# Heads of a delta-rule attention packed as 64-row blocks, with one PSUM bank per head, and another backward pass in the scheduler

## The chip, the cores and the metric

The kernel runs on one core of one Trainium2 chip. The metric is the device time of one launch in microseconds, the median of 3 runs. The engines are PE (TensorE; PEld is its weight loading), DVE (VectorE), ACT (ScalarE), POOL (GpSimd) and SP (SyncE, which issues all the DMAs here).

## What is computed

A delta-rule attention over 4 x 8 heads of 768 tokens and 48 features, then two MLPs over the 3072 tokens, 384 to 2048 to 384 features. Everything is float32.

```python
def _attn_ref(q, k, v, beta):
    k_n = k / (np.linalg.norm(k, axis=-1, keepdims=True) + 1e-06)
    state = np.zeros((B, H, D, D))
    for t in range(S):
        kt, vt, bt = k_n[:, :, t], v[:, :, t], beta[:, :, t, None]
        y[:, :, t] = np.einsum('bhd,bhde->bhe', q[:, :, t], state)
        v_old = np.einsum('bhde,bhd->bhe', state, kt)
        state = state + bt[..., None] * np.einsum('bhd,bhe->bhde', kt, vt - v_old)

def _moe_ref(x, w_in, w_out):
    h = x @ w_in
    return np.where(h > 0, h, np.exp(np.minimum(h, 0)) - 1) @ w_out

def _moe2_ref(x, w_in, w_out, a, b):
    h = x @ w_in
    P = a[0] + a[1] * h + a[2] * h**2 + a[3] * h**3
    Q = 1 + abs(b[0]) * abs(h) + abs(b[1]) * h**2
    return (P / (Q + 1e-06)) @ w_out
```

## The kernel before

**The attention** works in 12 steps of 64 tokens, two steps to a window (WINS, 6 windows). A step has 32 heads, in two halves `hf` of 16. In a half, 8 columns `u` times two heads `h` lie in the partitions, and the 64 tokens of a head are two blocks of 32. Per step the small PE groups are these (the names in bold are those of the profile):

- **gp** (`g_item`, 4 items per window): the products k·k and k·q of a head, 32 matmuls of 48 rows by 32 columns, 128 wide. DVE masks out `p`; three ACT copies per half put the diagonal blocks into `gd` and the block below the diagonal into `lo`.
- The inversion of the 32 x 32 triangles on DVE (`t_pieces`): a transpose `am<-gd`, the norms, then a chain of a product into `tmp` and a sum out of it (`merge`), and a transpose into `tp_t`, once per window for 32 blocks in 128 partitions.
- **ks** (64 matmuls of 48 x 32): the state times k; DVE subtracts it from `kv`, which POOL has scaled (`prep`), into `R`.
- **cb** three times: `solve(0)` with `tp_t`, `lo` with the block below the diagonal, `solve(1)`. ACT copies between them, DVE subtracts.
- `u2`: ACT copies the solution twice per half into `ub`, each time through a mask `mh_sb` that keeps one of two heads; `s_bd`, the state, has a block of zeros beside each head's state for the same reason.
- **y** (`yy`, per half): 8 matmuls of 128 x 64, 96 wide, with the state and 8 with `ub`, into one bank; a copy `y1`, three transposes **xt** (`xx`), and a copy into `xs`.
- **ku** (per half, 16 matmuls of 128 x 48): the update of the state, which DVE adds into `s_bd` by head.

The attention's PSUM tiles come from one ring of three banks, `pa`; a tile waits until the one three places ahead of it was read.

**The MLPs** are PE groups of 9 matmuls of 128 x 128, 512 wide (kind `F` in the code; `h`, `h_a`, `h_b`, `h_c` and `o` in the profile). The first MLP runs by windows, `H` and `O` of 16 feature tiles, among which the small groups of the next window are put; then the second MLP has PE to itself. `split_x` makes the high and low part `xh` and `xl` of a window's `xs`, and the window's first `H` waits for them. The weights come as float64 words and are converted on ACT, DVE and POOL (`conv_x`, `conv_d`, `conv_s`: the DVE operations `wo<-wo` and `ce<-wo`, 192 wide, of the first 140 us).

**What sets the order.** Every operation is recorded with its dependencies; `order` then runs a list scheduler over them, whose `simulate` has tables of durations (`PEC`, `LEAVE`, `ENTER`, `PAIR` for PE's groups, `SLACK` for the DMAs), and whose `backward` hands back to the next round how late an operation may be. The best of 8 rounds is written out as a fixed order for each engine. While PE waits ahead of the first F group, `gaps` puts matmuls named `fill` (L1478) into its queue, as many as the scheduler thinks fit; they have no dependency, but what stands behind them waits for them. `start` issues the first loads: `gin` tiles (two DMAs each, 48 partitions, 2 KB runs) for gp, then the rest.

In the profile all recorded operations have line 193, that of the recorder's `emit`, so tiles are read by their names.

Of the kernel before, what the change touches and what calls it, by code (L numbers as in the profile page):

```python
# [20 lines left out]
D = 48  # L21
NSC = 12
# [8 lines left out]
NV = 7  # L31
# [5 lines left out]
    wm1=6, wk=4, wr=3, wr0=4)  # L37


class View:  # L40
# [62 lines left out]

    def real(self):
        a = self.base.get()
        for c in self.chain:
            if c[0] == "[]":
# [67 lines left out]
class Recorder:  # L175
    def __init__(self, nc):
        self.nc, self.ops, self.group, self.live = nc, [], None, False
# [81 lines left out]
    def dma(self, out, in_):  # L259
        v = out if isinstance(out, View) else in_  # L260
        n = v.ids.size * 4 * (v.part[1] - v.part[0])
        self.add("SP", self.nc.sync.dma_start, dict(out=out, in_=in_), [out], [in_], SLACK["issue"], 2000, n)
# [44 lines left out]
    "F": (226.7, 425), "gp": (27.3, 475), "ks": (13.4, 330), "so": (22, 220), "lo": (22, 250), "yy": (85, 262), "ku": (47, 263),  # L307
    "xx": (90, 405), "wm": (200, 500), "yt": (33, 260)}
LEAVE = {"F": 2040, "so": 774, "lo": 812, "ks": 960, "gp": 970, "ku": 855, "yy": 1471, "xx": 290, "wm": 500, "yt": 1400}
ENTER = {"F": 0, "so": 71, "ks": 71, "xx": -25, "ku": 70, "yy": 20, "gp": 60, "lo": 100, "wm": 50, "yt": 20}  # L310
PAIR = {
# [3 lines left out]
SIZE = {"F": 9, "yy": 16, "yt": 48}  # L315
SLACK = {"small": 150, "F": 100, "x": 30, "issue": 560, "rate": 240, "land": 2300, "wait": 1500, "space": 3900, "room": 290, "first": 432, "hold": 400, "jit": 300, "pj": 0}
MIX = [
    (1076044, 1), (92414181, 200), (90150106, 200), (77610261, 20), (97147800, 60), (84287398, 200),
    (75730493, 60), (8425654, 600),
]  # L320

# [15 lines left out]
def order(ops, rounds):  # L337
# [17 lines left out]
    for _ in range(rounds):  # L355
# [3 lines left out]
        backward(ops, end)  # L359
# [5 lines left out]
def gaps(first):  # L365
    out, last = {}, None
    for o in first:
# [3 lines left out]
        if g.kind == "F":  # L371
            break
        if last is not None:
            n = len(last.ops) / SIZE[last.kind] if last.kind in SIZE else 1.0
            idle = o.start - last.ops[0].start - pe_cost(last.kind, "gp") * n - 300
            if idle > 430 and o.start > 20000:
                out[o] = int(idle / 430)
        last = g
# [7 lines left out]
def simulate(ops):  # L386
# [96 lines left out]
    while done < total:  # L483
# [10 lines left out]
        if e == "PE":  # L494
# [8 lines left out]
            if mode is not None:  # L503
                stop = began + pe_cost(mode, u.kind) * size
                t = max(t, stop)
                if u.kind == "F":
                    fill = False
                clock(began, t if fill else stop, t)
                if fill and t > max(stop, 20000) + 500:
# [4 lines left out]
                    while count > SLACK["first"] + 254.6 * used[0]:  # L514
                        used[0] += 1
            mode, began = u.kind, t
# [30 lines left out]
def backward(ops, end):  # L547
    nxt = end
    for o in sorted(ops, key=lambda o: (-o.start, -o.n)):
# [4 lines left out]
        if o.eng == "PE":  # L554
            late = nxt = min(late, nxt - o.pitch)
# [6 lines left out]
def kernel(  # L562
    ctx: ExitStack,
    tc: tile.TileContext,
    c_kq: bass.AP,
# [3 lines left out]
    mask_h: bass.AP,  # L569
# [988 lines left out]
```

## Time and profile before

| | |
|---|---|
| median of 3 runs (lowest, highest) | 1002.0 us (1001.04, 1003.21) |
| the profiled execution: its time, its span | 1002.51 us, 1000.7 us |
| PE busy | 982.7 us (98%), 10402 matmul records |
| DVE, ACT, POOL busy | 846.6, 753.1, 382.5 us |
| mean granted TensorE clock | 0.997 |
| DMA | 96.77 MB, mean 97 GB/s |

The span is the time from the first to the last instruction of the profiled execution; 1.8 us of its time lie around it. A float32 matmul has two records on PE, so a group of 32 shows x64; the F groups' matmuls have one each. A row of the timeline merges instructions of one kind that follow each other: its first number is the start, its second the time from there to the end of the last. Since PE's matmuls overlap, the time that a group takes is best read from its start to the next group's start. All the rows stand in their own section below.

### The profile page before, as it was taken

How to read it: one execution, taken by the hardware profiler on the slowest of the kernel's cores; microseconds unless marked ns; L12 is line 12 of the kernel's file. 1: busy time of each engine (PE TensorE's matmuls, PEld its weight loads, DVE VectorE, ACT ScalarE, POOL GpSimd, SP SyncE). 2: the span in 40 equal slices, each digit the busy share in tenths (PEclk: the TensorE clock that was granted, in tenths of full speed). 3: DMA queues.
4: the chain of work that ended last, by engine and by line, in shares of the span. 5: the costliest groups of instructions: out<-in, count | busy, mean ns of one | idle time of the engine just before them, and what ended most of it. 6: DMA issues, size and time to landing. Idle time of an engine off the chain costs nothing.

```text
span 1000.7 us, 25423 instructions
## 1 busy us (share of the span) xinstructions
PE 982.7 (98%) x10402; PEld 801.3 (80%) x10402; DVE 846.6 (85%) x1218; ACT 753.1 (75%) x1524; POOL 382.5 (38%) x282
## 2 busy tenths in 40 slices
PE   6999999999999999999999999999999999999997
PEld 4877878877887887788888888888888888888885
DVE  3999969987995998799666477889999999999996
ACT  3779799887877887887788778676676676766763
POOL 2353546542331242223222244364363643633332
PEclk9999999999999999999999999999999999999998
DMA  9554074226426432641545932001010010000000
GB/s 236 141 166 156 20 216 140 64 82 209 139 66 184 146 115 77 183 139 64 163 121 187 357 125 79 1 23 42 0 64 1 1 64 1 32 1 0 32 1 31
DMA packets 61588, 96.77 MB, mean 97 GB/s; under 512 B 7072, under 2 KB 39968, under 8 KB 61472
## 3 DMA queue, kind: packets, MB, share of 16 engines
q1 hardware_dynamic: 61472, 95.15, 30.4%
q8 instruction: 81, 1.33, 0.6%
q14 instruction: 35, 0.29, 0.1%
HBM read 73.11 MB, written 22.02 MB: 95 GB/s over the span
## 4 chain that ended last, share of the span: by engine, by line
PE 95%; DVE 2%; ACT 1%; issue 1%; DMA 0%; SPq 0%; ACTq 0%; DVEq 0%
PE o L193 39%; PE h L193 19%; PE h_b L193 10%; PE h_a L193 9%; PE fill L1478 4%; PE cb L193 3%; PE y L193 3%; PE gp L193 3%; PE ku L193 1%; PE ks L193 1%; PE h_c L193 1%; PE xt L193 1%; ACT wo L193 1%; DVE wo L193 1%; DMA wo<-c_kq 0%
## 5 line engine op out<-in xcount | busy, mean ns | idle before, releaser
L193 POOL TENSOR_TENSOR wor<-wo,wor 128x384 fp32r<-128x384 f32 x96 | 114.9, 1199 | 283.9 <-ACT wor L193 260.3
L193 POOL TENSOR_TENSOR gl<-wo 128x1024 fp32r<-128x1024 f32 x47 | 138.8, 2953 | 189.1 <-DVE wo L193 142.8
L193 PE MATMUL o<-gh,wor 128*128 128x512 f32 x576 | 195.1, 396 | 0.0
L193 PE MATMUL h<-xh,wi 128*128 128x512 f32 x546 | 185.5, 398 | 0.0
L193 ACT ACTIVATE wo<-wo 128x1024 f32<-128x1024 f32 (+3 forms) x224 | 142.3, 672 | 41.9 <-DVE wo L193 37.8
L193 PE MATMUL o<-gh,wo 128*128 128x512 f32 x576 | 139.7, 391 | 0.0
L193 PEld LDWEIGHTS o<-gh,wor 128*128 128x128 f32 x576 | 108.1, 188 | 23.9 <-issue 0.2
L193 PEld LDWEIGHTS o<-gh,wo 128*128 128x128 f32 x576 | 108.9, 189 | 22.7
L193 PEld LDWEIGHTS h<-xh,wi 128*128 128x128 f32 x546 | 102.4, 188 | 23.1 <-issue 0.6
L193 PE MATMUL o<-gl,wor 128*128 128x512 f32 x288 | 112.2, 390 | 0.0
L193 PE MATMUL h<-xl,wi 128*128 128x512 f32 x273 | 106.4, 390 | 0.3 <-DVE xl L193 0.3
L193 DVE SCALAR_TENSOR_TENSOR e<-e,pe 128x512 f32<-128x512 f32 x96 | 74.4, 775 | 37.4 <-ACT e L193 36.6
L193 DVE SCALAR_TENSOR_TENSOR wo<-wo 128x192 int32<-128x192 int32 (+2 forms) x101 | 87.4, 869 | 17.9 <-ACT wo L193 17.6
L193 PE MATMUL h_b<-xh,wi 128*128 128x512 f32 x300 | 96.4, 389 | 0.0
L193 DVE TENSOR_TENSOR gl<-e,gh 128x512 fp32r<-128x512 f32 x88 | 74.1, 843 | 20.2 <-ACT gh L193 19.9
L193 PE MATMUL h_a<-xh,wi 128*128 128x512 f32 x276 | 88.9, 389 | 0.0
L193 ACT ACTIVATE wo<-h_b,ab_sb 128x1024 f32<-128x1024 f32 (+1 forms) x52 | 57.3, 1128 | 33.5 <-PE h_b L193 33.5
L193 PE MATMUL o<-gl,wo 128*128 128x512 f32 x288 | 73.8, 391 | 2.0 <-DVE gl L193 2.0
L193 ACT ACTIVATE e<-h 128x512 f32<-128x512 f32 x91 | 54.4, 597 | 27.1 <-PE h L193 25.8
L193 DVE SCALAR_TENSOR_TENSOR gh<-wo,ab_sb 128x1024 fp32r<-128x1024 f32 (+1 forms) x49 | 63.3, 1293 | 7.5 <-ACT wo L193 1.7
L193 ACT ACTIVATE wo<-h_a,ab_sb 128x1024 f32<-128x1024 f32 x46 | 52.0, 1161 | 21.2 <-PE h_a L193 19.7
L193 ACT ACTIVATE wor<-wo 128x384 fp32r<-128x384 f32 x96 | 50.3, 524 | 21.6 <-PE o L193 19.6
(125 smaller groups left out, 2037.8 us busy)
## 6 DMA issues: line engine op xcount, KB each, us to landing
kq<-c_kq SPq DMA_DIRECT2D x22, 512.0 KB, 4.5
kv<-c_kv SPq DMA_DIRECT2D x24, 384.0 KB, 4.7
raw<-w_out SPq DMA_DIRECT2D x42, 192.0 KB, 2.7
gin<-c_kq SPq DMA_DIRECT2D x36, 192.0 KB, 3.8
raw<-w_in SPq DMA_DIRECT2D x34, 192.0 KB, 2.9
o2d<-cs SPq DMA_DIRECT2D x32, 192.0 KB, 2.5
i2d<-cs SPq DMA_DIRECT2D x32, 192.0 KB, 2.7
wi<-i2d SPq DMA_DIRECT2D x16, 384.0 KB, 3.3
```

What stands on the lines that cost most here:

```text
L193: fn(**{k: v.real() if isinstance(v, View) else v for k, v in kw.items()})
L1478: nc.tensor.matmul(out=wt["w"][:, 0:256], lhsT=c[:, 128:256], rhs=c, start=True, stop=True)
```

## The change

- **Layout.** The two blocks of a head now lie side by side: partition 64h + 32(block xor hf). `ks` then needs one matmul of 64 columns where it had two of 32; `lo` reads its block from the same tile `gl_` as the diagonal blocks, which one ACT copy per half fills (`gd`, `lo` and their three copies go). For gp there is a second copy of k and q in DRAM, `c_kg`, whose halves are crossed for `hf` = 1; its second block's moving operand is read as two windows of 64 columns that overlap.
- **No masks.** `ub` is one plain copy per half, and the state `s_st` has no zero blocks. `ku` works on 64 rows, and one DVE operation per half updates the state. `y` runs per head: 16 matmuls of 48 or 64 rows by 64 columns, 48 wide, with the state and 16 with `ub`, each head into a bank of its own, so `yy` takes two `pa` tiles, and two copies make `y1`. The copies of `solve(0)`'s result go by head (32 partitions), in the first window partly on DVE.
- **Loads.** A `gin` tile is one DMA of 128 partitions. `start` puts the first 8 weight loads behind the first window's tiles, and 4 `kv` tiles and the rest behind them; the second step's `kv` lies in the `wor` ring. The second and third gp item get banks that are free then.
- **Scheduler.** New entries for gp, ks and yy and another DMA rate (240 to 385). `backward` adds to PE's due times the cost of passing from a group to one of another kind, keeps the distance of groups behind the first F, and pushes the end by a number per round (`PUSH`). `gaps` also fills ahead of the first F group. `evac1` puts the first MLP's result through the ring `pe` instead of `ub`.

```diff
...
-SLACK = {"small": 150, "F": 100, "x": 30, "issue": 560, "rate": 240, "land": 2300, "wait": 1500, "space": 3900, "room": 290, "first": 432, "hold": 400, "jit": 300, "pj": 0}
+SLACK = {"small": 150, "F": 100, "x": 30, "issue": 560, "rate": 385, "land": 2300, "wait": 1500, "space": 3900, "room": 290, "first": 432, "hold": 400, "jit": 300,  "pj": 0}
...
+PUSH = [12000, 15000, 13000, 10000, 13000, 18000, 16000, 16000]
...
-    for _ in range(rounds):
+    for push in PUSH:
...
-        backward(ops, end)
+        backward(ops, end, push)
...
         if o.eng == "PE":
-            late = nxt = min(late, nxt - o.pitch)
+            g, d = o.group, o.pitch
+            if after is None:
+                late = min(late, o.start) - push
+            elif after.group is not g:
+                k = len(g.ops) / SIZE[g.kind] if g.kind in SIZE else 1
+                d = max(d, pe_cost(g.kind, after.group.kind) * k - o.off)
+                if o.start > wide:
+                    d = max(d, after.start - o.start)
+            late = nxt = min(late, nxt - d)
+            after = o
...
-                for h in range(2):
-                    rows = slice(64 * h, 64 * h + D)
-                    rc.dma(out=t[rows], in_=c_kq[s, :, rows, 4 * bb:4 * bb + 4, :].rearrange("f p u n -> p f (u n)"))
-                gin_t[s, bb] = t, not park
+                t = t.rearrange("p (u n) -> p u n", u=8)
+                rc.dma(out=t, in_=c_kg[s, hf])
+                gin_t[s, hf] = t, not park
...
     def grp(hf, h, blk):
-        o = 32 * ((2 * blk + h) ^ (3 * hf))
+        o = 64 * h + 32 * (blk ^ hf)
...
+        if i == 1:
+            ps = h_s
+        elif i == 2:
+            ps = [po.tile([128, 512], F32, tag=t, name="gp") for t in ("o1", "o2")]
...
+                        mm(out=ps[hf][grp(hf, h, blk), u % 4], lhsT=k[:, 32 * blk:32 * blk + 32],
+                           rhs=k[:, 32:128].windows(64, 32) if blk else k, start=True, stop=True)
...
-            act(out=gd[b0, u0:u0 + 4], in_=ps[hf][b0, :, 0:32], func=AF.Copy)
-            act(out=gd[b1, u0:u0 + 4], in_=ps[hf][b1, :, 32:64], func=AF.Copy)
-            act(out=lo_t[b0, 4 * bb:4 * bb + 4], in_=ps[hf][b0, :, 32:64], func=AF.Copy)
+            act(out=gl_t[:, u0:u0 + 4], in_=ps[hf][:, :, 0:64], func=AF.Copy)
...
+                            mm(out=ps[hf][o:o + 64, u], lhsT=d["kq"][o:o + D, u, 0:64],
+                               rhs=s_st[o:o + D, 8 * hf + u], start=True, stop=True)
...
+                        if w == 0 and hf == 1:
+                            vector.tensor_copy(out=d["R"][rs], in_=d["cb"][rs])
+                        else:
+                            act(out=d["R"][rs], in_=d["cb"][rs], func=AF.Copy)
...
-                    ub = ap2.tile([128, 8, 2, D], F32, tag="ub", name="ub")
-                    d["ub"] = ub
-                    for h in range(2):
-                        act(out=ub[:, :, h], in_=d["cb"], func=AF.Copy, scale=mh_sb[:, h ^ hf:(h ^ hf) + 1])
...
+                    d["ub"] = ap2.tile([128, 8, D], F32, tag="ub", name="ub")
+                    act(out=d["ub"], in_=d["cb"], func=AF.Copy)
...
-                y = pa.tile([128, DM], F32, tag="pa", name="y")
+                y = [pa.tile([128, 4, D], F32, tag="pa", name="y") for _ in range(2)]
...
+                            out = y[h][64 * bl:64 * bl + 64, i]
+                            if part == 0:
+                                mm(out=out, lhsT=d["kq"][o:o + D, v, 64:128], rhs=s_st[o:o + D, 8 * hf + v], start=(i == 0), stop=False)
+                            else:
+                                mm(out=out, lhsT=p_d[s][o:o + 64, 8 * hf + v], rhs=d["ub"][o:o + 64, v],
+                                   start=(s == 0), stop=(s == 0 or i == 3))
...
+                        mm(out=ps[rs, u], lhsT=d["kv"][rs, u, 0:64], rhs=d["ub"][rs, u], start=True, stop=True)
...
+                xs = mp.tile([128, 512], F32, tag="pe", name="xe")[:, 0:NC]
...
-        gin_ahead(NV)
+        gin_ahead(3)
         load_beta(0)
-        rc.dma(out=mh_sb, in_=mask_h)
+        conv_loads(Q["wl"])
+        rc.behind = rc.sent
+        for _ in range(4):
+            ch_ahead("kv")
+        gin_ahead(4)
...
```

What the change moves, at three places. Rows are those of the built programs, in the order in which they stand on one engine; the shape is that of the output (of a matmul: columns of the weights x width), and x32 means 32 such instructions in a row.

SP at the start of the program, before (`wo_86` is a part of the weights' tile that holds the first window's gp inputs for a while, `xg` two more such places):

```order
L193 DMA wo_86<-c_kq 48x2x512 x2
L193 DMA cm_sb<-mask_p 128x256
L193 DMA wo_86<-c_kq 48x2x512 x4
L193 DMA xg<-c_kq 48x2x512 x2
L193 DMA bl<-beta_l 128x32
L193 DMA xg<-c_kq 48x2x512 x4
L193 DMA gin<-c_kq 48x2x512 x4
L193 DMA kv<-c_kv 128x768 x2
```

and after:

```order
L198 DMA wo_84<-c_kg 128x1024 x3
L198 DMA cm_sb<-mask_p 128x256
L198 DMA xg<-c_kg 128x1024
L198 DMA bl<-beta_l 128x32
L198 DMA wo_84<-w_in 128x384 x8
L198 DMA xg<-c_kg 128x1024 x2
L198 DMA gin<-c_kg 128x1024 x2
L198 DMA kv<-c_kv 128x768 x2
```

The first window's four inputs were eight DMAs of 48 partitions, ahead of only four more; they are four of 128 partitions now, and the first 8 weight loads stand ahead of the second window's inputs.

DVE in the inversion of the first window (`tmp` products and the sums out of them), before:

```order
L193 TENSOR_TENSOR tmp<-tt 128x256
L193 TENSOR_REDUCE tt<-tmp 128x4x2x8
L193 TENSOR_TENSOR tmp<-tt 128x512
L193 SCALAR_TENSOR_TENSOR wo_86<-wo_86 128x192
L193 TENSOR_REDUCE tt<-tmp 128x4x2x8
L193 SCALAR_TENSOR_TENSOR wo_86<-wo_86 128x192
L193 TENSOR_TENSOR tmp<-tt,am 128x1024
L193 SCALAR_TENSOR_TENSOR ce<-wo_86 128x192
L193 TENSOR_REDUCE tt<-tmp 128x64
```

and after:

```order
L198 TENSOR_TENSOR tmp<-tt 128x256
L198 TENSOR_REDUCE tt<-tmp 128x4x2x8
L198 TENSOR_TENSOR tmp<-tt 128x512
L198 TENSOR_REDUCE tt<-tmp 128x4x2x8
L198 SCALAR_TENSOR_TENSOR ce<-wo_84 128x192
L198 TENSOR_TENSOR tmp<-tt,am 128x1024
L198 SCALAR_TENSOR_TENSOR ce<-wo_84 128x192
L198 TENSOR_REDUCE tt<-tmp 128x64
```

Weight conversions and masks `p` stood between the steps of the inversion; here none does ahead of the 1024 wide product. Over the whole inversion, from the transpose `am` to the transpose `tp_t`, 22 conversions and 8 masks stood among its steps, and now 11 and 7.

PE at the end of the second window's attention, before (all of it stands in one row between an `h` and an `o` group; names with the built program's numbers, which tell the two halves apart):

```order
L193 MATMUL h0_1468<-xh_1421,wi14_2548 128x512
L193 MATMUL y_2707<-s_bd_95,kq_2062 64x96 x8
L193 MATMUL y_2707<-ub_2681,p_471 64x96 x8
L193 MATMUL y_2740<-s_bd_95,kq_2204 64x96 x8
L193 MATMUL y_2740<-ub_2692,p_471 64x96 x8
L193 MATMUL xt_2771<-cm_sb_91,y1_2751 128x128 x3
L193 MATMUL ku_2778<-ub_2681,kv_2159 48x48 x16
L193 MATMUL ku_2799<-ub_2692,kv_2240 48x48 x16
L193 MATMUL xt_2826<-cm_sb_91,y1_2775 128x128 x3
L193 MATMUL o0_1551<-gh_2638,wor_2742 128x512
```

and after (`h` and `o` are F groups):

```order
L198 MATMUL y<-s_st,kq 64x48 x16
L198 MATMUL y<-ub,p 64x48 x16
L198 MATMUL h_138<-xh,wi_2422 128x512
L198 MATMUL h_138<-xl,wi_2422 128x512
L198 MATMUL h_138<-xh,wi_2422 128x512 x2
L198 MATMUL h_138<-xl,wi_2422 128x512
L198 MATMUL h_138<-xh,wi_2422 128x512 x2
L198 MATMUL h_138<-xl,wi_2422 128x512
L198 MATMUL h_138<-xh,wi_2422 128x512
L198 MATMUL y<-s_st,kq 64x48 x16
L198 MATMUL y<-ub,p 64x48 x16
L198 MATMUL xt<-cm_sb,y_2686 128x128 x3
```

The two halves' outputs now stand on either side of an F group, and `ku` behind another. From the first F group on, PE's row had 68 such visits to small groups, and has 80 now, with the same number of groups of each kind: 20 `y`, 20 `cb` with `tp_t`, 10 with `lo`, 10 `ks`, 15 `gp`, 18 `ku`, 20 `xt`, and 384 F groups. Ahead of the first F group there were 93 `fill` matmuls, 61 of them in one row ahead of the first `cb`; now there are 75, of which 34 and 25, parted by one gp group, stand ahead of the first `cb`.

## Rows read from the trace of the kernel before

**Rows 1.** Page, parts 1 and 4: busy time by engine; last chain by engine.
```profile
PE 982.7 (98%) x10402; PEld 801.3 (80%) x10402; DVE 846.6 (85%) x1218; ACT 753.1 (75%) x1524; POOL 382.5 (38%) x282
...
PE 95%; DVE 2%; ACT 1%; issue 1%; DMA 0%; SPq 0%; ACTq 0%; DVEq 0%
```

**Rows 2.** Chain in order of time: start us, us, what.
```profile
690.35 4.08 PE h_a L193 x18
```

**Rows 3.** Timelines of ACT, PE, POOL: first two steps, to the first F.
```profile
62.93 2.00 ACT L193 ACTIVATE ub<-cb,mh_sb 128x384 f32<-128x384 f32 x4 [0.60 <-PE cb L193]
...
69.05 1.69 PE L193 MATMUL ks<-s_bd,kq 48*32 48x48 f32 x128
...
70.28 0.83 POOL L193 TENSOR_TENSOR kv<-kv,n_t 128x384 f32<-128x384 f32 x1 [2.14 <-DMA kv<-c_kv]
...
73.46 1.20 PE L193 MATMUL cb<-R,tp_t 32*32 32x48 f32 x64
...
88.86 0.50 PE L193 MATMUL h<-xl,wi 128*128 128x512 f32 x1 [0.26 <-DVE xl L193]
```

**Rows 4.** Timeline, PE, start to first solve: start us, us, what, [idle before].
```profile
4.75 1.96 PE L193 MATMUL gp<-wo 48*32 48x128 f32 x62 [0.34 <-DMA wo<-c_kq]
...
27.50 1.16 PE L193 MATMUL gp<-gin 48*32 48x128 f32 x64
...
31.16 26.60 PE L1478 MATMUL fill<-cm_sb 128*128 128x256 f32 x122
...
57.69 1.05 PE L193 MATMUL cb<-kv,tp_t 32*32 32x48 f32 x64
```

**Rows 5.** Timeline, DVE, inversion of the first window.
```profile
19.05 1.96 DVE L193 STREAM_TRANSPOSE am<-gd 128x1024 f32<-128x1024 f32 x1 [0.81 <-ACT gd L193]
...
28.67 0.42 DVE L193 TENSOR_TENSOR p<-gp,cm_sb 128x256 f32<-128x256 f32 x1 [1.13 <-PE gp L193]
...
34.54 0.41 DVE L193 TENSOR_TENSOR tmp<-tt 128x256 f32<-128x256 f32 x1
...
34.98 0.42 DVE L193 TENSOR_REDUCE tt<-tmp 128x64 f32<-128x256 f32 x1
...
41.01 0.34 DVE L193 SCALAR_TENSOR_TENSOR wo<-wo 128x192 int32<-128x192 int32 x1
...
41.28 0.94 DVE L193 TENSOR_REDUCE tt<-tmp 128x64 f32<-128x768 f32 x1
...
55.36 2.02 DVE L193 STREAM_TRANSPOSE tp_t<-am 128x1024 f32<-128x1024 f32 x1
```

**Rows 6.** DMA view, 0 to 40 us in 40 slices; one issue line.
```profile
GB/s 0 39 277 195 232 195 168 164 197 198 200 199 201 209 219 229 203 217 212 340 411 431 386 374 401 396 371 87 22 16 307 209 254 167 287 170 186 11 0 18
...
wo<-c_kq SPq DMA_DIRECT2D x6, 192.0 KB, 4.6
```

**Rows 7.** Timeline, PE, 105 to 133 us: small groups among F groups.
```profile
105.18 1.38 PE L193 MATMUL ks<-s_bd,kq 48*32 48x48 f32 x128
...
116.93 0.88 PE L193 MATMUL cb<-R,tp_t 32*32 32x48 f32 x64
...
117.74 0.50 PE L193 MATMUL o<-gh,wor 128*128 128x512 f32 x1
...
120.02 0.88 PE L193 MATMUL cb<-R,lo 32*32 32x48 f32 x64
...
127.28 0.88 PE L193 MATMUL y<-s_bd,kq 128*64 128x96 f32 x16
...
128.75 0.50 PE L193 MATMUL h<-xh,wi 128*128 128x512 f32 x1
...
132.10 0.92 PE L193 MATMUL ku<-ub,kv 128*48 128x48 f32 x32
...
132.95 0.49 PE L193 MATMUL o<-gh,wor 128*128 128x512 f32 x1
```

**Rows 8.** Timeline, DVE: last step of the second inversion.
```profile
113.90 2.13 DVE L193 STREAM_TRANSPOSE tp_t<-am 128x1024 f32<-128x1024 f32 x1
```

More of the change, by code (lines that the diff above doesn't have):

```diff
@@ L102, in to_broadcast, with windows @@
         return self._with(np.broadcast_to(self.ids, shape[1:]), ("to_broadcast", shape))
+    def windows(self, n, step):
+        a = [self.ids[i:i + n] for i in range(0, len(self.ids) - n + 1, step)]
+        return self._with(np.stack(a), ("windows", n, step, len(a)))
     def real(self):
@@ L176, in __init__ @@
     def __init__(self, nc):
-        self.nc, self.ops, self.group, self.live = nc, [], None, False
+        self.nc, self.ops, self.group, self.live, self.behind, self.sent = nc, [], None, False, None, None
     def brk(self, kind):
@@ L261, in dma @@
         n = v.ids.size * 4 * (v.part[1] - v.part[0])
-        self.add("SP", self.nc.sync.dma_start, dict(out=out, in_=in_), [out], [in_], SLACK["issue"], 2000, n)
+        o = self.add("SP", self.nc.sync.dma_start, dict(out=out, in_=in_), [out], [in_], SLACK["issue"], 2000, n)
+        if self.behind is not None:
+            o.deps.setdefault(self.behind, "s")
+        self.sent = o
     class Eng:
@@ L334, in mixed, with order @@
     return draw(MIX[0][0], n)
-def order(ops, rounds):
+def order(ops):
     groups = []
@@ L515, in simulate @@
                         used[0] += 1
+            fill = fill and u.kind != "F"
             mode, began = u.kind, t
@@ L544, in simulate, with backward @@
     return end
-def backward(ops, end):
-    nxt = end
+def backward(ops, end, push=0):
+    nxt, after = end, None
+    wide = min(o.start for o in ops if o.group is not None and o.group.kind == "F")
     for o in sorted(ops, key=lambda o: (-o.start, -o.n)):
@@ L735 @@
     gin_t = {}
-    gin_q = [(w, j, s, bb) for w in range(NW) for j, s in enumerate(WINS[w]) for bb in range(2)]
+    gin_q = [(w, s, hf) for w in range(NW) for s in WINS[w] for hf in range(2)]
     gin_n = [0]
@@ L1054, in yy @@
-                for u in range(8):
-                    bl, i = u % 2, u // 2
-                    if w == 0 and u == 4:
-                        warm(d["ub"][:, 0, 0, 0:16], Q[f"wm{j}"])
-                        rc.brk("yy")
-                    mm(out=y[64 * bl:64 * bl + 64, 96 * i:96 * i + 96], lhsT=p_d[s][:, 8 * hf + 4 * bl + i],
-                       rhs=d["ub"][:, 4 * bl + i].rearrange("p a b -> p (a b)"), start=(s == 0), stop=(s == 0 or i == 3))
-                y1 = d["y1"] = ap2.tile([128, DM], F32, tag="y1", name="y1")
@@ L1067, in xx @@
+                if s > 0:
+                    ch_ahead("kq")
+                y1 = d["y1"] = ap2.tile([128, DM], F32, tag="y1", name="y1")
+                for h in range(2):
+                    o = y1.rearrange("p (i h n) -> p i h n", i=4, h=2)[:, :, h]
+                    if s == 0:
+                        vector.tensor_copy(out=o, in_=y[h])
+                    else:
+                        act(out=o, in_=y[h], func=AF.Copy)
             def xx(hf, j=j, st=st):
@@ L1338, in start @@
     def start():
[L1339 to L1340 removed]
         gin_ahead(1)
         rc.dma(out=cm_sb, in_=mask_p)
[L1343 removed]
+        gin_ahead(3)
         load_beta(0)
[L1345 removed]
+        conv_loads(Q["wl"])
[3 more added lines that the diff above has]
+        gin_ahead(4)
     def chain_loads():
[L1348 to L1350 removed]
+        for _ in range(2):
+            ch_ahead("kq")
         conv_ahead()
+        rc.behind = None
     def coefs():
@@ L1468 @@
         fn(*a)
-    _, first = order(rc.ops, 8)
+    _, first = order(rc.ops)
     idle = gaps(first)
```

193 lines of the change are left out of this document (80 added, 113 removed), and 4 rows, old and new, of the table PAIR.

## Prediction

> **What bounds the kernel now.** I read the page first, then the chain that ended last. PE is busy in 98% of the span and holds 95% of the chain [rows 1], so time is what PE's row of work costs, plus what PE spends on waiting, or on `fill` in place of waiting, ahead of the first F group. The chain in order of time shows the rest: from 88.86 us on it runs on PE alone, and where nothing stands between, two F groups take 4.08 us, 2.04 each [rows 2]. The program has 384 of them before and after, some 783 us that the change doesn't touch. Two parts are left. One is the front, from 0 to the second matmul of the first F group at 88.86 us [rows 3]. The other is what the small groups add to PE's row behind it. The end of the kernel is not touched.
>
> In the front I then read PE's timeline: the first gp group runs at 4.75 us (but for its first two records), the last of the fills that cover the first inversion ends at 57.76, and the first `cb` starts at 57.69 [rows 4]. So the front has three pieces: loads and gp up to the transpose `am<-gd` at 19.05, the inversion on DVE from there to the end of `tp_t` at 57.38 [rows 5], and the two steps of the first window from 57.69 to 88.86 [rows 3, 4].
>
> **Loads and gp.** The reader is to see the rate in the DMA view: some 200 GB/s up to 18 us, where DMAs of 48 partitions run, and 340 to 430 between 19 and 26, where those of 128 partitions do [rows 6]. The first gp item needed 0.39 MB; it will need two tiles, 1.05 MB. Data begins to move at 2 us; at 400 GB/s the two tiles are there 2.6 us later, and with the lag of about 1 us that the first item shows (0.39 MB moved by 3.4, gp at 4.75) gp starts at 5.6. At 200 it would be 8.2. I take 400, since the new DMA has 128 partitions. The four items take about 2.1 us each at this place (62 records in 1.96 us; 64 take 1.16 later [rows 4]), and since items two and three have banks of their own, none waits for an evacuation: 14.0. Two ACT copies and the hand-over behind them I estimate at 1.4, since weight conversions stand among them now; so the transpose starts at 15.4, not 19.05: **-3.6 us** (at 200 GB/s -1.0).
>
> **The inversion.** 22 conversions and 8 masks stood in it, now 11 and 7. A conversion costs the next one's start 0.27 us (41.01 to 41.28) [rows 5]; but it hides 0.11, because a sum that follows its product directly starts 0.44 after it where the product itself takes 0.41 (34.54 to 34.98), and 0.33 with something between, when the next operation may start some 0.08 ahead of its end [rows 5]. So 11 x 0.16 = 1.8 us go, 0.3 with one mask, and the wait of 1.13 us for gp that a mask had in this row [rows 5], because the gp items come sooner. **-3.2 us**, so `tp_t` ends at 50.6 (19.05 - 3.6 + 38.3 - 3.2). PE can't start `cb` before its fills are through: 59 of them at 26.60 / 61 = 0.436 [rows 4] and a gp of 1.16 take 26.9 us behind the seventh gp item (1.1), which follows the mask of the sixth; by the sum of the steps in between that is at 22, so 50.0. The two agree, and I take 50.8 for `cb`, **-6.9 us** in all.
>
> **The first two steps.** The window from `cb` to the end of `ks` took 13.05 us (57.69 to 70.74) [rows 3, 4]. Two copies of `ub` instead of four are worth 1.0 us there (2.00 for four [rows 3]); against it stands the transpose of the next window, now ahead of the subtraction of `lo` on DVE, +1.0, and the banks: `yy` takes two of three `pa` banks, so the second half waits for copies of the first, +0.6. From the end of `ks` to the next `cb` 2.72 us passed (70.74 to 73.46), because POOL had waited 2.14 us for `kv` [rows 3]; `kv` is loaded early now and what is left are two subtractions, 1.2: -1.5. From that `cb` to the F groups I find 15.0 for 15.4: one copy of `ub` less, but the copies of `y`'s second half stand behind six conversions on ACT, and `ku` needs the banks that they free. Sum **-1.3 us**; the front then ends at 80.7, 8.2 us sooner. The fills agree with a shorter front: 18 fewer.
>
> **The small groups among the F groups.** A visit's price is read from start to start. `cb`, 32 matmuls of 32 x 32 in 64 records, takes 0.81 us (116.93 to 117.74), and F plus `cb` 3.09 where F alone is 2.04 and `cb` 0.81: a visit costs 0.24 beside its groups [rows 2, 7]. Twelve more visits: **+2.9 us**.
>
> `y`: 1.47 us per half (127.28 to 128.75), 20 halves. The new one has 32 matmuls, 48 wide, of 64 x 64. `ku` is the nearest row: 16 matmuls, 48 wide, on two parts of the array, 0.85 us (132.10 to 132.95) [rows 7]. The order of `yy` takes four parts in turn (two row halves, two column halves), and each head has its bank, so I take twice the number in the same 0.85, which is just over what 32 matmuls need at all in `cb`. 20 x 0.62 = **-12.4 us**. If only two parts run at a time it is 1.70, +4.6 us in place of that; `cb` at 0.81 is the other end.
>
> `ks`: 64 matmuls of 32 columns on eight parts took 1.31 (1.38 [rows 7] less the 0.07 by which `cb`'s 0.88 is over its 0.81). Now 32 of 64 columns on two parts, like twice `ku`, 1.70: 10 x 0.39 = **+3.9 us**; at the pace of `cb` it would be -5.0.
>
> gp: the same number of matmuls of the same shape, on the same eight parts; the windows change where operands come from. 0, no gain possible since the columns are as many; 15 x 0.16 = +2.4 if half of the group ran a quarter slower (1.16 for 64 records [rows 4]). The copies on ACT and DVE become fewer and are covered by PE's row. `cb`, `ku`, `xt` keep their count.
>
> **Waits of PE in the row.** Before there were none. The second inversion ends at 116.03 [rows 8], 0.90 us ahead of its `cb` at 116.93 [rows 7]. By DVE's order it loses some 4 us of work, but `cb` comes one F group sooner behind a front that is 8 us shorter, measured from a transpose that starts about 5 sooner; I allow one F group of waiting, **+2.0 us**.
>
> **The sum.** -6.9 - 1.3 + 2.9 - 12.4 + 3.9 + 2.0 = -11.8, so the profiled execution of 1002.5 us becomes 990.7. The median of the runs lies 0.5 below that execution, so I predict **990.2 us**.
>
> A rule of the Trainium skill speaks against splitting `y`: "TensorE: Matmul & The Clock Gate", section "Wait — 56ns, not 53.3ns?", says that start-to-start never drops below about 25 ns however narrow a matmul is. By it the 64 records of a new `y` half would take 1.6 us, and 15 us of the gain would be gone, about 1005. The trace disagrees: `cb` has 64 records in 0.81 us, 12.7 ns each [rows 7].
>
> **Rivals.** *The parts don't overlap (slower).* What decides is whether a matmul in the upper row half and one in the lower run at once into two banks of the same partitions. If not, a `y` half takes 1.70 us, 20 x 0.85 = 17 more, 1007.2, slower than before. The change stops paying at a half of 1.44 us (0.85 + 11.8 / 20). For it: no `y` or `ku` row shows four parts. Against it: gp has eight parts, which are two row halves times four column quarters, and does 32 matmuls of 128 columns in 1.16 us [rows 4], 36 ns each, while `y`'s of 96 columns on two parts take 92 (16 in 1.47 [rows 7]). Chance 0.05.
>
> *The count of records sets the pace.* If `y`'s spacing stayed what it is (32 records in 1.47, 46 ns [rows 7]), 64 would take 2.9 us, 20 x 2.1 = 42 more, 1032. `cb` with 12.7 ns and `ks` with 10 (128 records in 1.31) speak against it. Chance 0.01. At the floor of that page of the Trainium skill this rival would give about 1005.
>
> *PE waits at the windows' edges.* By PE's order the last `xt` now stands one or two F groups ahead of the `H` that reads it, where it stood three or four, and `evac1` puts three tiles through the ring of `pe`, which the next window's ACT work needs. One F group of waiting at each of five edges is 10.2 us, 1000.4, in reach of no change. For it: the order itself, and DVE and ACT at 846.6 and 753.1 us [rows 1]. Against it: the scheduler puts waits into its order, and before PE had none. Chance 0.09.
>
> *The front doesn't shrink.* If the loads come at 200 GB/s and the weight conversions that now stand ahead of the transpose hold it up, `cb` starts where it did: 990.2 + 6.9 = 997.1. Chance 0.06.
>
> **How the numbers follow.** Forecast 0.79. Its own bounds: without the waits in the row, and with `ks` at half its extra, 986; with another 1.5 us of `cb` at 50.8 and gp at +2.4, 994. With the front rival and most of the edges the range is 984 to 1000; the slower rivals and the last of the edges stay outside. A measurement can tell about 0.2%, 2 us. Faster: 0.79 + 0.06 + half of the edges, 0.89; same: the other half, 0.05; slower 0.06.
>
> **What would show it.** The first `cb` on PE at about 51 us and the first F group at about 81; the sums in the inversion directly behind their products; `y` at about 0.85 us from start to start, with two visits per step, `ks` at 1.7; F groups at 2.04; no idle time on PE ahead of `cb`, `h` or `y` behind the front. A `y` of 1.7, or idle rows on PE at the edges with `xl` or ACT as releaser, would make the prediction wrong, and a DMA rate of 200 GB/s ahead of the first gp would move the front.

## Result, and the profile after

The changed kernel takes **1013.7 us** (median of 4 runs, 1011.8 to 1018.1), the one before 1002.3 beside it: 1.012 times as long, with a 95% interval of 1.0085 to 1.0156. The forecast was 990.2. The profiled execution has 1012.8 us and a span of 1011.0, 10.3 more than before: the first F group starts at the same time (88.05 us for 88.09, its second matmul 0.4 us sooner), and from the first to the last F group, which I call the row, 918.2 us pass for 907.7.

The page, against [rows 1], with busy times and the chain that ended last:

```profile
PE 983.7 (97%) x10398; PEld 800.8 (79%) x10398; DVE 848.3 (84%) x1202; ACT 737.5 (73%) x1446; POOL 371.7 (37%) x280
...
PE 91%; DMA 3%; DVE 3%; ACT 2%; issue 2%; POOL 0%; SPq 0%; ACTq 0%; DVEq 0%; POOLq 0%
```

PE's share of the chain falls from 95 to 91%, and DMA, DVE, ACT and "issue" (waiting for nothing that the profile shows) take its place. The timeline of PE in the front, against [rows 3, 4], where the last bracket is the idle time ahead and what ended it:

```profile
5.74 1.74 PE L198 MATMUL gp<-wo 48*32 48x128 f32 x54 [0.65 <-DMA wo<-c_kg]
...
13.60 0.37 PE L198 MATMUL gp<-xg 48*32 48x128 f32 x1 [2.42 <-issue]
...
23.03 1.44 PE L198 MATMUL gp<-xg 48*32 48x128 f32 x34 [2.05 <-issue]
24.40 2.07 PE L1483 MATMUL fill<-cm_sb 128*128 128x256 f32 x4
...
54.81 0.88 PE L198 MATMUL cb<-kv,tp_t 32*32 32x48 f32 x64
...
73.79 0.88 PE L198 MATMUL cb<-R,gl__158 32*32 32x48 f32 x64 [2.12 <-ACT R L198]
...
87.35 0.42 PE L198 MATMUL gp<-gin 48*32 48x128 f32 x8 [1.54 <-issue]
...
88.46 0.39 PE L198 MATMUL h<-xl,wi 128*128 128x512 f32 x1
```

gp starts when it was forecast (5.74 for 5.6), but three gp groups stop in their middle for 6.0 us in all, released by nothing that the profile shows. At the end of the first of them the granted clock falls to 0.50 and stays there for 13.7 us. The table by stretches has the length, PE's busy time, the granted clock (1.00 is 2.4 GHz, 0.50 is 1.2 GHz), the DMA share and GB/s:

```profile
12.00:16.00 4.00, 1.49 (x37) 0.69 1.04 405
16.00:20.00 4.00, 2.43 (x76) 0.50 1.03 407
20.00:24.00 4.00, 1.95 (x59) 0.50 1.02 394
76.00:80.00 4.00, 3.35 (x135) 0.70 0.19 53
192.00:196.00 4.00, 4.00 (x14) 0.69 0.00 2
```

The four fill records at 24.40 took 2.07 us; at full clock 122 took 26.60 [rows 4]. On DVE, against [rows 5], the inversion starts at 16.34 and waits 2.20 us for the gp group that had stopped:

```profile
16.34 2.05 DVE L198 STREAM_TRANSPOSE am<-gl__158 128x1024 f32<-128x1024 f32 x1
...
24.22 0.42 DVE L198 TENSOR_TENSOR p<-gp,cm_sb 128x256 f32<-128x256 f32 x1 [2.20 <-PE gp L198]
...
50.99 2.00 DVE L198 STREAM_TRANSPOSE tp_t<-am 128x1024 f32<-128x1024 f32 x1
```

In the row, PE's timeline against [rows 7]:

```profile
104.69 2.07 PE L198 MATMUL ks<-s_st,kq 48*64 48x48 f32 x64
106.69 0.50 PE L198 MATMUL h<-xh,wi 128*128 128x512 f32 x1
...
129.74 0.68 PE L198 MATMUL y<-s_st,kq 48*64 48x48 f32 x32
130.24 0.65 PE L198 MATMUL y<-ub,p 64*64 64x48 f32 x32
130.82 0.50 PE L198 MATMUL o<-gh,wor 128*128 128x512 f32 x1
...
136.21 1.14 PE L198 MATMUL ku<-ub,kv 64*64 64x48 f32 x32
137.27 0.50 PE L198 MATMUL o<-gh,wor 128*128 128x512 f32 x1
```

From start to start `ks` takes 2.00 us (1.31 before), a half of `y` 1.08 (1.47), `ku` 1.06 (0.85). And PE's waits behind the front (us, times, longest), of which before had the first alone:

```profile
PE o L198 <- DVE gl L198: 2.0, 1, 2.0
PE ks L198 <- ACT gl__2992 L198: 1.5, 1, 1.5
PE xt L198 <- DVE s_st L198: 1.3, 1, 1.3
PE o L198 <- ACT xe L198: 0.6, 1, 0.6
PE h L198 <- DVE xl L198: 0.2, 1, 0.2
```

### The profile page after: what moved, and what is told of

It reads as the page before. It is cut to its first block, busy times and chain, and to the rows that moved or that the text cites. A ratio compares the mean times of both kernels' runs of the same rounds, so it can differ in the third digit from the quotient of the medians.

```text
span 1011.0 us, 25255 instructions
## 1 busy us (share of the span) xinstructions
PE 983.7 (97%) x10398; PEld 800.8 (79%) x10398; DVE 848.3 (84%) x1202; ACT 737.5 (73%) x1446; POOL 371.7 (37%) x280
## 3 DMA queue, kind: packets, MB, share of 16 engines
q8 instruction: 81, 1.33, 0.5%
## 4 chain that ended last, share of the span: by engine, by line
PE 91%; DMA 3%; DVE 3%; ACT 2%; issue 2%; POOL 0%; SPq 0%; ACTq 0%; DVEq 0%; POOLq 0%
PE o L198 38%; PE h L198 18%; PE h_b L198 10%; PE h_a L198 9%; PE fill L1483 3%; PE cb L198 3%; PE gp L198 2%; PE ks L198 2%; PE y L198 2%; PE ku L198 2%; PE xt L198 1%; PE h_c L198 1%; DMA x2d<-xe 1%; DVE wo L198 1%; DMA o2d<-cs 1%
## 5 line engine op out<-in xcount | busy, mean ns | idle before, releaser
L198 POOL TENSOR_TENSOR wor<-wo,wor 128x384 fp32r<-128x384 f32 x96 | 111.3, 1161 | 286.7 <-ACT wor L198 281.1
L198 PE MATMUL o<-gh,wor 128*128 128x512 f32 x576 | 198.0, 400 | 0.6 <-ACT xe L198 0.6
L198 ACT ACTIVATE wor<-wo 128x384 fp32r<-128x384 f32 x96 | 50.1, 522 | 22.4 <-PE o L198 21.6
```

What stands on the lines that cost most here:

```text
L198: fn(**{k: v.real() if isinstance(v, View) else v for k, v in kw.items()})
```

## Experiments

Theories: **W**, matmuls with 64 stationary columns are dearer; **I**, PE outruns its instructions where small matmuls follow one another without a pause, and the clock falls behind the wait; **O**, the new order has waits that the old one had not. Times are medians, with the interval of the ratio to the kernel before, run beside each (1001.8 to 1003.2 us); a seed (`MIX`) breaks ties in the order, so that each order made anew has its own chance waits; first F and row, in us, are those of the profiled execution, which in e2_ks32 was the longest of four (1017.9 us) and in b_all32b the shortest (1007.5 us), so that their rows are not those of the median.

| kernel | us | ratio to before | first F | row |
|---|---|---|---|---|
| before | 1002.3 | | 88.1 | 907.7 |
| after | 1013.7 | 1.0085 to 1.0156 | 88.0 | 918.2 |
| e1_ku48 | 1019.5 | 1.0153 to 1.0212 | 90.5 | 922.8 |
| e2_ks32 | 1012.8 | 1.0080 to 1.0148 | 87.4 | 923.8 |
| f_fills | 1010.2 | 1.0045 to 1.0100 | 86.7 | 919.3 |
| l_late | 1017.3 | 1.0133 to 1.0195 | 87.5 | 923.5 |
| c_fills2 | 1008.7 | 1.0036 to 1.0082 | 84.2 | 917.2 |
| c_fills_ks32 | 1011.9 | 1.0076 to 1.0124 | 84.5 | 920.3 |
| s_old_in_after | 1019.4 | 1.0153 to 1.0190 | 94.9 | 917.4 |
| s_new_in_before | 1010.1 | 1.0059 to 1.0096 | 89.0 | 913.8 |
| n_ks_cost | 1010.1 | 1.0057 to 1.0094 | 84.5 | 918.3 |
| r_evac | 1009.2 | 1.0054 to 1.0101 | 88.5 | 913.4 |
| p_front_a | 1005.0 | 1.0018 to 1.0036 | 91.1 | 908.1 |
| p_front_b | 1005.4 | 1.0020 to 1.0044 | 89.6 | 908.0 |
| b_all64 | 1009.6 | 1.0050 to 1.0094 | 83.5 | 917.3 |
| b_all32 | 1016.2 | 1.0103 to 1.0184 | 91.8 | 918.2 |
| b_all32b | 1017.3 | 1.0070 to 1.0180 | 86.4 | 914.5 |

### The width of the stationary operand

```diff
 # e1_ku48, emitted in the place of each ku matmul and of its sum
-matmul(out=ps[64*h:64*h+64, u], lhsT=kv[rs, u, 0:64], ...)
-tensor_tensor(out=s_st, in0=s_st, in1=ps, op=add)
+matmul(out=ps[64*h:64*h+48, u], lhsT=kv[rs, u, 0:48], ...)
+for o in (0, 64): tensor_tensor(out=s_st[o:o+48], in0=s_st[o:o+48], in1=ps[o:o+48], op=add)
 # e2_ks32, in the place of each ks matmul
-matmul(out=ps[hf][o:o+64, u], lhsT=kq[o:o+48, u, 0:64], ...)
+for b in (0, 32): matmul(out=ps[hf][o+b:o+b+32, u], lhsT=kq[o:o+48, u, b:b+32], ...)
```

> The changed kernel with ku's matmuls 48 columns of kv wide again, as before, on the same two quarters of the array, and ku's sum on VectorE in two halves of 48 rows; the order of all engines is that of the changed kernel. Theory A, the width of the stationary operand is the price: a ku group that took 1.065 us in the row (0.855 before) goes back to about 0.855, so 18 groups in the row give 3.8 us and four in the front up to 0.8: about 1009.5. Rival B, the price is that the two matmuls stand on two row halves of 64 rows and not on 128 rows: ku stays at 1.06 and the time at 1013.7.

> The changed kernel with each 64-column matmul of ks cut into two of 32 columns, next to each other on the same quarter of the array (64 matmuls a group instead of 32); the order of all engines is that of the changed kernel. Theory A, what a matmul costs beside its moving columns goes with the width of its stationary operand, and two column quarters run at once: ks falls from 2.09 us to 1.4 to 1.7, ten groups give 4 to 7 us, 1007 to 1010. Rival B, the matmuls of one row half follow one another whatever their columns: 64 of them take 3.0 us or more, 1022 or later.

Timelines of PE, first of e1_ku48, then of e2_ks32:

```profile
139.56 0.92 PE L961 MATMUL ku<-ub,kv 64*48 64x48 f32 x32
140.41 0.50 PE L199 MATMUL o<-gh,wor 128*128 128x512 f32 x1
```

```profile
105.49 1.56 PE L962 MATMUL ks<-s_st,kq 48*32 48x48 f32 x128
106.98 0.50 PE L199 MATMUL h<-xh,wi 128*128 128x512 f32 x1
...
344.15 0.50 PE L199 MATMUL h<-xl,wi 128*128 128x512 f32 x1 [2.81 <-issue]
```

Theory A of both holds in the step itself: `ku` is back at 0.85 us on the same two quarters, so there the width alone is the price, and `ks` is at 1.49. The matmuls of e2_ks32 are narrower and stand on more parts of the array at once; which of the two makes the gain, it doesn't tell apart. The instructions' view of weight loads agrees: a median of 106 ns with 32 columns (`ks` before), 125 with 48 (`ku` before, 128 rows), 135 with 64. The Trainium skill, "TensorE: Matmul & The Clock Gate", section "LDWEIGHTS (loading the stationary operand)", says that the load goes with the columns and not with the rows; the trace agrees for the rows (137 ns for 128 rows of 64 columns in `y` before, 135 for 64 rows in `ku` after), and for the columns up to 64, while the 128 columns of `xt` take no more than 140.

The totals missed, each for its own reason. e1_ku48 is 6 us slower than the changed kernel, since DVE now has two sums per `ku` of 0.55 us each, and PE waits for it and what stands behind it (1.3 and 0.2 us in the changed kernel):

```profile
PE xt L199 <- DVE s_st L969: 3.9, 3, 2.0
PE h L199 <- DVE xl L199: 2.7, 5, 1.1
```

So the 16 columns of padding had paid for one DVE operation instead of two; the change's own choice was the better one. In e2_ks32 5 us of cheaper `ks` came back as waits, the longest of them the 2.81 us inside an F group, with no releaser.

### The front, and PE without instructions

```diff
 # f_fills: fill matmuls ahead of the front's gp groups; c_fills2: six more
+idle = {gp 3: 3, gp 4: 3, gp 5: 2, gp 6: 2}
+idle |= {last ku group but one: 3, last gp: 3}     # c_fills2
 # l_late, in start() and chain_loads()
-conv_loads(8); rc.behind = rc.sent; four times ch_ahead("kv")
+ch_ahead("kv") twice, behind the gp items
```

> The changed kernel with ten more fill matmuls on PE among the first six gp groups: three ahead of the third, three ahead of the fourth, two ahead of the fifth and of the sixth (0.44 us each at full clock, 4.4 us together). Theory A, PE ran out of instructions because the gp groups went through them faster than the next 16 KB of the instruction queue could land: work between them gives that time, the two waits of 2.42 and 2.05 us shrink to under 1 us together, the granted clock holds at full through the first 30 us, and the first cb comes at 52 to 54 us instead of 54.8; total 1011 to 1013. Rival B, the waits don't depend on how fast PE gets there: they stay at 2.4 and 2.0, and the fills come on top, first cb at 57 to 59 us, total 1016 to 1018.

> The changed kernel with the loads of the front where they stood before: no eight weight loads and no four kv loads right behind the first gin tiles, two kq and two kv after the gp items, and no wait between loads. Theory A, PE outruns its instruction queue whatever else is loaded: the two waits of 2.42 and 2.05 us among the gp groups stay within 0.6 us of that, and the front gets longer by the wait for kv (about 1.5 us): 1014 to 1017. Rival C, the early loads at 350 to 400 GB/s hold up the 16 KB of instructions: without them the two waits fall under 1 us together, the first cb comes at 51 to 52.5 and the total at 1010 to 1013.

> The changed kernel with the ten fills of the run before and six more: three ahead of the ku group at 82 us and three ahead of the last gp group before the first F, where PE waited 1.5 to 2.5 us without a releaser. Theory A, PE outruns its instructions there too: the fills take the place of the wait, the granted clock holds to the first F group, which starts at 85 to 86.5 us; total 1007 to 1010. Rival B, the wait stays and the fills come on top: first F at 88.5 to 90 us, total 1011 to 1014.

PE's timeline of f_fills:

```profile
53.40 1.00 PE L198 MATMUL cb<-kv,tp_t 32*32 32x48 f32 x64 [0.41 <-DVE p L198]
...
85.00 1.10 PE L198 MATMUL gp<-gin 48*32 48x128 f32 x28 [2.48 <-issue]
```

c_fills2 by stretches, and its first F group:

```profile
12.00:16.00 4.00, 4.00 (x136) 1.00 1.04 408
16.00:20.00 4.00, 3.41 (x76) 1.00 1.03 399
76.00:80.00 4.00, 4.00 (x113) 1.00 0.82 219
```

```profile
84.23 0.59 PE L198 MATMUL h<-xh,wi 128*128 128x512 f32 x1
```

Ten fills, 4.4 us of additional work, made both early waits vanish and `cb` 1.4 us sooner; six more took the third wait away, and the first F group came at 84.2: theory I. In the totals only the sixteen fills stand clear of the changed kernel; the interval of the ten overlaps with its own. The clock, full where it had been 0.50, was not quite held as expected: in c_fills2 it was 0.50 for 3.4 us from 22.4 us, behind a wait of 1.52 us for ACT. In l_late the three waits were 1.27, 0.47 and 1.91 us (2.42, 2.05 and 1.54 in the changed kernel), and neither theory's numbers held. But the run doesn't try rival C: other loads moved up, and some 400 GB/s ran beside the first wait in both kernels. PE went on at 13.60, as in the changed kernel, and only came later to the place where it stopped:

```profile
13.60 0.37 PE L198 MATMUL gp<-xg 48*32 48x128 f32 x1 [1.27 <-issue]
```

Its row, in an order of its own, is 5 us longer by other waits.

What PE lacked is seen in the DMA view: the instruction queue moves 16 KB at a time, here in the second from 11 us, in which the first wait begins (packets, MB, share):

```profile
q8 instruction: 1, 0.02, 7.1%
```

By the trace's DMA records that packet ran from 11.27 to 12.40, and PE went on at 13.60. In all 27 waits without a releaser of over 1 us, in twelve of these kernels, before among them, PE went on 1.2 to 1.6 us after such a packet had ended; of moments spread evenly over the first 350 us, 5 in 100 lie so. The place settles it: counted in the order of their starts, weight loads and the sequencer's instructions included, the matmul behind each of the 27 waits is PE's instruction 194 or 195 behind a multiple of 256 (450, 706 and 3010 in the changed kernel), and so it is behind all 24 shorter waits of this kind of over 0.2 us, while PE's waits for other engines and DMAs stand at many places. So PE stops at one fixed place of every 256 instructions, and a packet is about as many: the changed kernel has 81 of them for 20883 instructions of PE. The packets at the waits took 0.88 to 1.19 us, with 17 to 419 GB/s beside them, which speaks against rival C. The Trainium skill, "Runtime: NRT & Kernel Launch", section "Instruction fetch mechanics", has blocks of 16 KiB (256 instructions) that are fetched while the last is executed, and the fetch hidden because instructions are issued more slowly than it fills; the trace agrees with the block and differs in the rest, for groups of small matmuls.

### The order and the layout apart

```diff
 # s_old_in_after: order, gaps, backward, simulate of the kernel before
-def order(ops): ... for push in PUSH: ... backward(ops, end, push)
+def order(ops, rounds): ... for _ in range(8): ... backward(ops, end)
 # s_new_in_before: the reverse, in the kernel before
 # n_ks_cost: c_fills2's fills, and in the tables
-"ks": (47, 330)   "ks": 1600   MIX = [(91438583, 1), ...]
+"ks": (57, 330)   "ks": 1905   MIX = [(15960800, 1)]
 # r_evac: c_fills2's fills, and in evac1
-xs = mp.tile([128, 512], F32, tag="pe", name="xe")
+xs = mp.tile(... tag="pe" ...) if c < 2 else ap1.tile([128, 512], F32, tag="xe", name="xe")
```

> The new layout with the order's passes (simulation, backward pass, gaps, eight rounds) of the kernel before; seeds and costs are those of the changed kernel. Theory L, the layout makes the loss (ks and ku dearer by 10 us in the row, gp outrunning its instructions in the front): ks stays at 2.09, ku at 1.06, two or three waits of PE of 1.5 to 2.5 us without a releaser stay in the front, and the time stays at 1010 to 1020. Rival S, the new backward pass makes the loss, since its order holds waits that the order before had not: without it PE's waits in the row (3.4 us and 1.7 for the clock in the changed kernel) go, and the time is 1003 to 1009.

> The layout of the kernel before with the new passes (simulation, backward pass with its eight pushes, gaps) in the order; seeds and costs are those of the kernel before. Theory L, the layout makes the loss: the time stays at 999 to 1005, with ks at 1.40 and PE's waits in the row under 3 us together. Rival S, the new pass makes it: waits of PE in the row of 3 us and more, 1006 to 1012.

> The changed kernel with the sixteen fills of the front, and with the order made anew with ks's cost as measured (1.9 us a group in the table instead of 1.6) under another seed, whose order has no visit of gp and ks together. Theory W, the waits in the row come from the order (ks right behind gp waits 1.46 us for ACT's copies, and 3.4 us at half clock follow): they go, and with the fills it is 1004 to 1007. Rival N, an order made anew brings other waits of PE of the same size: 1008 to 1013.

> The changed kernel with the sixteen fills of the front, and the third of the three copies at each window's end in a tile of its own, as before, instead of in the ring of pe, where it takes the place of the first copy and waits for that to land in memory; the order is nearly that of the run with the fills alone (three F groups and one xt moved). Theory R, the ring holds up the third copy, and with it the first O group of the next window: no wait of PE for xe any more (0.70 us with the fills alone, 0.59 in the changed kernel), 1006 to 1008.5. Rival N, the wait comes from ACT's own row: PE still waits 0.5 to 2 us for xe, and the time stays at 1008 to 1011.

With the old passes the row stays at 917.4 and `ks` and `ku` at their price: theory L. The new passes together (the run doesn't part the backward pass from the simulation and the fills) are worth 6.8 us in the front of the new layout; in the old one they made an order in which PE waits, above all here (s_new_in_before):

```profile
PE cb L193 <- DVE tp_t L193: 3.5, 1, 3.5
```

so there the rival's case holds, and the change loses by either part, as far as one order of each can show it. In n_ks_cost the visit of gp and `ks` is gone and so is its wait, but 1.5 us for `xe` and 1.5 without instructions stand in other places: N. r_evac took the wait for `xe` out as theory R has it (0.7 us in c_fills2, 1.5 in n_ks_cost, 2.1 in s_old_in_after, none here): its row has the full clock throughout and is the shortest of the new layout, 913.4. Of the 3.8 us by which it is shorter than that of c_fills2, though, only 0.7 are that wait: its own order has an F group between gp and `ks`, and with it the wait of 1.46 us for ACT and the half clock behind it are gone. Its front, at 88.5, gave that back, so its total stands where rival N had it.

### Everything repaired at once, and the front's part alone

```diff
 # b_all64: c_fills2's fills, r_evac's tile, n_ks_cost's table, MIX = [(37000656, 1)]
 # b_all32, b_all32b: the same with e2_ks32's matmuls, "ks": (42, 330), 1400, two seeds
 # c_fills_ks32: c_fills2 with e2_ks32's matmuls
 # p_front_a, p_front_b: in the kernel before, two seeds, "rate" 385 for 240, and in gin_ahead and g_item
-for h in range(2): rc.dma(out=t[rows], in_=c_kq[s, :, rows, 4*bb:4*bb+4])
+rc.dma(out=t, in_=c_kq[s, :, :, 4*bb:4*bb+4])
-ps = [pa.tile(...) for _ in range(2)]
+ps = h_s if i == 1 else [po.tile(...) for t in ("o1", "o2")] if i == 2 else [pa.tile(...) for _ in range(2)]
```

> The same sixteen fills and ks cut into matmuls of 32 columns, which took 1.59 us a group instead of 2.09 when it was done alone. Theory A, the two gains add: 5 us less than with the fills alone, 1003 to 1006. Rival I, the 64 more records in each ks group make PE run out of instructions at other places (as the wait of 2.8 us inside an F group did when ks was cut alone): waits without a releaser of 2 us or more in the row, half clock behind them, 1007 to 1012.

> The changed kernel with all repairs that leave its matmuls as they are: sixteen fills in the front, the third copy at a window's end in a tile of its own, ks's measured cost in the table, an order made anew under a seed that has no visit of gp and ks together. If the named causes are all: first F at 84 to 86 us as with the fills, the row from the first to the last F group at 913 to 915 us as in the run with the copy's own tile, 1002 to 1005. If something else holds it: a front over 88 or a row over 916, 1007 or more.

> As b_all64 with ks in matmuls of 32 columns (1.59 us a visit instead of 2.09) and that cost in the table, under a seed of its own. If the narrow ks pays where nothing else waits: the row at 908 to 910, 998 to 1001, level with the kernel before or below it. If PE runs out of instructions behind ks wherever it stands: two or three waits of 1.5 to 2.5 us without a releaser in the row, 1003 to 1008.

> As b_all32 under a second seed: the same two cases with the same numbers; the difference of the two says what an order's chance is worth.

> The kernel before (its layout, masked copies and y as they were) with two things of the front alone: the gp items loaded over all 128 partitions in one DMA each, and items two and three in banks of their own; its order is made anew with a load rate of 385 instead of 240 GB/s in the table and another seed. Theory F, this part of the change pays by itself, because gp starts sooner and waits for no copies: first F at 85 to 87 us instead of 88.1, nothing dearer in the row, 998 to 1001. Rival I, gp without its waits runs through its instructions too fast here too: waits without a releaser of about 2 us among the gp groups, half clock behind them, first F at 88 or later, 1002 to 1006.

> As p_front_a, under a second seed, to see how much of its time is the order's chance: by theory F within 2 us of p_front_a, by rival I at 1002 to 1006.

The narrow `ks` was eaten in all four kernels that have it. PE's waits in c_fills_ks32:

```profile
PE ks L962 <- issue: 3.9, 2, 2.2
PE cb L199 <- issue: 2.5, 1, 2.5
PE h L199 <- issue: 1.9, 1, 1.9
```

b_all32 has 8.4 us of such waits and b_all32b, in its shortest run (1007.5), 5.4; both medians are above what either case said. Rival I holds: in these orders 64 more records a group cost at least what they save. The kernel before has 128 records in a `ks` group as well and no such wait in its row; its halves of `y` have 32 where these have 64. b_all64 has the shortest front, 83.5, and no wait for `xe`, but its order has a row of 917.3: the two gains were not had together, and what an order's chance is worth (913 to 924 in the row of the six kernels with `ks` and `ku` as changed and an order of their own) is as large as what was to be shown. This stays open. Nor does the front's part pay alone in the kernel before: the transpose starts sooner (15.33 and 16.13 for 19.05), yet the orders made anew bring the first `cb` later (60.66 and 59.51 us, for 57.69 in [rows 4]), in p_front_a with DVE behind a weight conversion:

```profile
60.66 1.11 PE L193 MATMUL cb<-kv,tp_t 32*32 32x48 f32 x64 [1.41 <-DVE wo L193]
```

Theory F failed; rival I's time held, but not by its mechanism (no wait without a releaser was over 1.4 us, and the clock stayed full). No kernel of these beats the one before.

## Why the prediction was wrong

| step | forecast | measured |
|---|---|---|
| loads and gp, to the transpose | -3.6 | -2.7 (16.34 for 19.05) |
| inversion, and PE's fills to `cb` | -3.2 | -0.2 (`tp_t` -1.7, then fills to 54.81) |
| first two steps | -1.3 | +2.5 |
| `y`, 20 halves | -12.4 | -7.1 (21.5 for 28.5) |
| twelve more visits | +2.9 | +3.3 (80 for 68) |
| `ks`, ten groups | +3.9 | +7.0 (2.00 for 1.31) |
| `ku`, 18 groups in the row | 0 | +3.9 (1.06 for 0.85) |
| gp | 0 | 0 |
| `xt`, 20 groups | 0 | -1.3 (6.1 for 7.4) |
| waits in the row | +2.0 | +3.6, and 1.6 at half clock behind one |

The terms of the row are sums over all groups of a kind, each from its start to the next group's start, with the waits and the half clock taken out; a visit is what the F groups beside it take over 2.04. The measured column sums to 10.6; the span grew by 10.3, since the end of the kernel, from its last wait on, is some 0.3 us shorter. Of the 22 us between forecast and measured, 12 are the prices of `y`, `ks` and `ku`, 8 are the front, and 3 are waits and clock in the row; `xt` gave 1 back.

**Loads and gp** was right in its mechanism: 400 GB/s, gp at 5.74. That its size came so near is in part luck: the first two items took 1.33 and 1.70 us instead of 2.1, and the next two stopped for 2.42. **The inversion and the two steps** failed where I moved every later step forward with gp and asked only for data, banks and engines. "None waits for an evacuation" was true; what stopped gp was its own instructions, which before had come in time but for 0.56 us, among waits of 1.2 to 1.5 us for ACT. DVE then waited 2.2 us, and the fills, a fixed number behind gp on PE, moved `cb` to 54.81 though `tp_t` ended at 52.99. In the two steps ACT's copy of `R` stood behind a weight conversion whose load had not landed (2.12 us), a third gp group ran out of instructions (1.54), and a `cb` at half clock took 1.50 us. On ACT in the changed kernel:

```profile
71.61 0.63 ACT L198 ACTIVATE wo<-wo 128x192 f32<-128x192 f32 x2 [0.94 <-DMA wo<-w_out]
...
72.76 0.97 ACT L198 ACTIVATE R<-cb 32x384 f32<-32x384 f32 x2
```

c_fills2 shows that 3.8 us of this front hung on instructions and clock (with them went 1.2 of the 2.12 us for `R`); the forecast of 80.7 was not reached by any kernel.

**`y`**: the price of 0.85 came from a `ku` with 48 stationary columns, while `y` has 64. At the price of the new `ku`, 1.06, the term is -8.2; a new half takes 1.08, and the rest of the miss is that ten of the old halves stood two in a row, at 2.79 for both instead of twice 1.47. So the four parts do run at once, the rival of parts that don't overlap (1.70) fell, and the step that failed is the row it was sized by. **`ks`** was sized by that same row, and at twice 1.06 would have come to +8. **`ku`** was costed at nothing because its count stays; its shape does not (48 columns to 64, which the diff shows). That is the plainest miss, 3.9 us. **Waits**: "Before there were none" leaves out the 2.0 us at the kernel's end, which both kernels have. The edge rival named the copies through the ring of `pe`; that wait is real (r_evac) but short, and the larger ones are `ks` right behind gp and the clock behind it. With only the cost of shapes and visits (7.0 + 3.9 + 3.3 - 7.1 - 1.3 = 5.8) the row would be 913.5; r_evac's, with its own 81 visits and 1.3 us of short waits, is 913.4.

The range failed because its ends were built from each term's own doubt, while three terms hung on one row, and because no rival had PE wait for its own instructions, though the trace of before shows it twice, at a gp and at a `cb`:

```profile
16.28 1.50 PE L193 MATMUL gp<-xg 48*32 48x128 f32 x39 [0.56 <-issue]
...
77.79 0.23 PE L193 MATMUL cb<-R,lo 32*32 32x48 f32 x1 [1.18 <-issue]
```

## What to carry to other kernels

A matmul's price goes with its shape on both sides: where a step keeps its count but its stationary operand gets wider, cost it anew, and size no term by a row of another width. Taking waits away from a run of small matmuls can make the engine run out of instructions; a few idle matmuls between them can then be cheaper than the wait and the half clock behind it. And see what padding buys elsewhere before cutting it: 16 columns of `ku` stood for a DVE operation that was on the path.

## What the hardware showed that I had not expected

- PE stops for 1.2 to 3.2 us when a run of small matmuls gets to the end of the instructions that are there, always at the same place of a block of 256, and goes on 1.2 to 1.6 us after a 16 KB packet of the instruction queue (27 waits). How long it stops depends on when it gets there: 11.18 us in the changed kernel and 12.33 in l_late, with the same end at 13.60.
- Behind five of the seven waits of over 1 us in the changed kernel (the one at its start left out) the granted clock was 0.50, for 3.4 to 13.7 us; an F group in such a stretch took 3.61 us (190.54 to 194.15) instead of 2.04. In b_all32b it stayed at 1.00 behind four waits of 1.3 to 1.9 us, and in s_old_in_after behind one of 2.88: the wait alone doesn't tell.
- A group of `ks` as 64 matmuls of 32 columns is shorter (1.49 us) than as 32 of 64 (2.00), although it has twice the records; in the kernel's time the gain was lost again.
